# A new written order, column halves and earlier weight loads in the first block of a fused attention, FFN and MoE kernel

## The chip, the cores and the metric

One core of one Trainium2 chip runs the whole program. The metric is device time in microseconds (us) of one execution, as a median of several runs. Engines: PE is TensorE, DVE is VectorE, ACT is ScalarE, POOL is GpSimd; SP only issues DMAs. Each engine works through its own queue of instructions strictly in order, and semaphores tie the queues together.

## What is computed

Sliding-window attention with a few global keys (2 batches, 8 heads, 768 tokens, head size 64), then an FFN with the gate h * tanh(softplus(h)), then four experts, weighted by probabilities. All inputs are float32, except the FFN's weights, which come as float64.

```python
scores = scale * np.matmul(q, k.transpose(0, 1, 3, 2))
keep = is_global | is_local          # 8 global keys, 96 local ones
scores = np.where(keep, scores + bias, -1e9)
a = np.exp(scores - np.max(scores, axis=-1, keepdims=True))
a = a / (np.sum(a, axis=-1, keepdims=True) + 1e-09)
x = np.matmul(a, v)                  # -> 1536 x 512
h = x @ w_in                         # 512 -> 2048
y = (h * np.tanh(np.log1p(np.exp(h)))) @ w_out
for e in range(4):                   # experts, 512 -> 1024 -> 512
    out += p[:, e:e + 1] * (np.maximum(y @ w1[e], 0.0) @ w2[e])
```

## The kernel before

The 1536 tokens are worked on in three blocks of 512. In blocks 1 and 2 attention is spread over the FFN and expert steps of the block before, and every matmul of the FFN and the experts is done in three products of split operands. The first block is different, and it is where the change lies: attention has nothing to hide behind there, and the block runs in plain float32 products (each matmul instruction shows as two records). Its attention is cut into 16 pairs of heads (`FirstPair`, four pairs for each 128 tokens; the first four look at 128 keys, the others at 256), and its FFN into 16 steps of 128 hidden units.

`first_block` (line 786 on) issues all this from a string, `PLAN`, one letter for each operation, taken from left to right. So the string is the order of every engine's queue. The letters, with the engine and the line in the profile:

- of a pair: S scores (PE, L355), X bias and row minimum (DVE, L264, two instructions), E exponential with row sum (ACT, L275, two), D reciprocals for two pairs (DVE, L366 and L367), N scaling by the reciprocal (POOL, L372, two), T transposes (PE, L192), C copy of the transposed tile out of PSUM by ACT (L382), Z the same by DVE (not used before), A values (PE, L391), and for each four pairs F or G, the copy of the result into `x0` by ACT or DVE (L396; G alone is used before)
- of the conversion of one FFN weight tile from float64 bits to float32: a (ACT, L584), then three t (DVE, L587, L589, L591; the last one also sends the tile to a DRAM copy, `wfirst`, through SP, L593)
- of an FFN step: H hidden product (PE, L750, 8 records), e, c, n, l, u, m, v, g the gate (e: ACT, L643; c and n: DVE, L650 and L657; l: ACT, L662 and L663; u, m, v, g: DVE, L667, L672, L678, L682), P projection (PE, L762, 8 records)
- w: a third of the splitting of an expert tile (ACT L609 for the first third, DVE L612 for the two others), Y: matmuls that keep PE busy, i: the loads for the next block's attention, j and 1 to 6: its first round.

H needs all 16 pairs copied into `x0` and the converted tile; P needs the gate's g. A FFN weight tile is loaded (1 MB) into one of four buffers, so the load of tile k is issued on SP when tile k-4 has been converted (`ahead`, L802, calls `fetch`, L557); the tiles 12 to 15 use only two of the buffers. SP's queue is in order too: a load stands behind the DRAM copies and loads that were put there before it. The first two tiles are loaded at the start, between the tiles of keys and queries (L131 to L137). The three expert tiles that the block needs at its end are loaded by the first w (L856).

The values lie in `vz` as 192 columns for each pair and 128 keys: 64 of the one head, 64 of zeros, 64 of the other. Each matmul of A takes 128 of them (L391), so both heads' products go to all 128 output rows and the zeros keep them apart. Scores, by contrast, use the array in two halves of 64 rows, one for each head.

The flag that chooses between the narrow and the general program is worked out from two integers, loaded by two DMAs, one on SP and one on ACT (L68, L69).

Of the kernel before, what the change touches and what calls it, by code (L numbers as in the profile page):

```python
# [41 lines left out]
PLAN = (  # L42
    "SSYXXESYSEXSEDXNXESNTDCTXSENANCTXESACTDEAXNSCNETXACTDEGANCSNaAXatTTtCSCAEXtAESDGNSXNTXEStTCDSEXNACNX"
    "EAtaTDTtNCSCANXEtAEtTTCGCADatNAaNtTtCTACtaAtGtHattteHacntlteHuamcvgnPetlctauHtmvngtlPteaucmHtvngtlPt"
    "eaucmHtvgntlPteaucmtHvngtlPteaucmtHvgntltPeucmtvHngtltPeucmtvHngtltaPeucmvngHtltautiPemcvgnPtltutHmw"
    "vwgwePwcnwlwHumvgePcnlHuwmwvwgeHcnlPuemcvngHlumvPegcnlPumvgj1P23456"
)
# [12 lines left out]
@with_exitstack  # L60
def fused_attention_ffn_moe(ctx: ExitStack, tc: tile.TileContext, qkv, qk, vz, q_t, k_t, v_n, nloc, nglob, wff, wts, probs, out):
    nc = tc.nc
# [4 lines left out]
    nw = const.tile([P, 2], I64, tag="nw", name="nw")  # L67
    nc.sync.dma_start(nw[:, 0:1], nloc.unsqueeze(0).broadcast_to([P, 1]))  # L68
    nc.scalar.dma_start(nw[:, 1:2], nglob.unsqueeze(0).broadcast_to([P, 1]))  # L69

# [61 lines left out]
    for n, raw in enumerate(raws):  # L132
        at = slice(P if n < 2 else 0, 3 * P)
        nc.sync.dma_start(raw[:, 0:6 * P].rearrange("p (n c) -> p n c", n=2)[:, :, at],
                          qk[2 * n:2 * n + 2, :, at].rearrange("n p c -> p n c"))
        if wff.dtype == I64 and n % 2:
            nc.sync.dma_start(big[n // 2].bitcast(I64), wff[n // 2])  # L137

# [183 lines left out]
class FirstPair(NarrowPair):  # L322
# [6 lines left out]
    def load(self):  # L329


        nc, body, n = self.nc, self.body, self.n // 2
        if self.n % 2 == 0:
            v = body.ring.tile([P, 1024], F32, tag="wl" if n % 2 else "wh", name=f"vz{n}")[:, 0:768]
            v = body.values = v.rearrange("p (n c d) -> p n c d", n=2, c=2)
            c = slice(2 - self.nk, 2)
            nc.sync.dma_start(v[:, :, c, :], body.vz[n][:, :, c, :])
            if n < len(body.raws):
                qk = body.raws[n]
            else:  # L340
                qk = body.wpool.tile([P, 1024], F32, tag="w", name=f"qk{n}")
            body.keys = qk[:, 0:6 * P].rearrange("p (n c) -> p n c", n=2)
            if n >= len(body.raws):
                nc.sync.dma_start(body.keys, body.qk[2 * n:2 * n + 2].rearrange("n p c -> p n c"))
        self.v = body.values[:, self.n % 2]
        self.k, self.q = body.keys[:, self.n % 2, 0:2 * P], body.keys[:, self.n % 2, 2 * P:3 * P]
# [21 lines left out]

    def scale(self):
        for j in range(2):  # L370
            p = self.p[:, j, 0:self.nk * P]
            self.nc.gpsimd.tensor_scalar(p, p, self.sum[:, j:j + 1], 0.0, ALU.mult, ALU.add)  # L372

# [10 lines left out]
    def av(self):  # L384

        body = self.body
        if self.pr == 0:
            body.o = body.bank(f"o{self.u}", 1)
        mms = [(c, j) for c in range(self.nk) for j in range(2)]
        for c, j in mms:  # L390
            self.nc.tensor.matmul(body.o[:, self.pr * P:(self.pr + 1) * P], self.v[:, 2 - self.nk + c, j * 64:j * 64 + P],  # L391
                                  self.pt[:, c * 256 + j * P:c * 256 + (j + 1) * P], start=(c, j) == mms[0], stop=(c, j) == mms[-1])

# [129 lines left out]
class Body:  # L523
# [33 lines left out]
    def fetch(self, s):  # L557

        kind, t, n = self.steps[s]
        if kind == "ffn" and self.wide and t == 0:  # L560
            self.w64[s] = (self.big + self.twice)[TURN[n]].bitcast(I64)
            if n > 1 or not self.loaded:
                self.nc.sync.dma_start(self.w64[s], self.wff[n])
            return
        if kind == "ffn" and self.wide and t > self.first:
            return
        self.w32[s] = self.wpool.tile([P, 1024], F32, tag="w", name=f"w{s}")
        self.nc.sync.dma_start(self.w32[s], (self.wts if kind == "moe" else self.wfirst if self.wide else self.wff)[n])
# [219 lines left out]
    def first_block(self, ready, now):  # L788
# [10 lines left out]
        for pair in pairs:  # L799
            pair.load()  # L800

        def ahead():  # L802
# [18 lines left out]

        def scale(k):
            assert n["D"] > k // 2
            pairs[k].scale()

# [6 lines left out]

        def hidden(s):
            assert n["F"] == 4 and n["t"] >= 3 * s + 3
            self.accumulating = True
            self.hidden_first(s)
            ahead()
# [14 lines left out]
        def part(k):  # L852
            c, third = divmod(k, 3)
            assert ready["fetch"] >= NF1 and n["S"] == len(pairs) and n["P"] >= 8 + 2 * c
            if third == 0:
                now("fetch", NF1 + 3)  # L856
                next(parts[c])
# [5 lines left out]
        def begin_next(k):  # L863
# [4 lines left out]
        ops = {  # L868
            "S": scores, "X": pair("biased"), "E": pair("exps"), "D": inverse, "N": scale, "T": pair("trans"),
            "C": pair("copy", nc.scalar.copy), "Z": pair("copy", nc.vector.tensor_copy), "A": pair("av"),  # L870
# [6 lines left out]
        }  # L877
        same = dict(Z="C", G="F")
        for token in PLAN:
# [170 lines left out]
```

## Time and profile before

| | us |
|---|---|
| median of 3 runs | 945.83 (945.04 to 948.88) |
| profiled execution, time | 944.16 |
| its span, first to last instruction | 942.3 |
| first H of the block starts | 49.23 |
| last P of the block ends | 167.7 |

The profiled execution has 1.86 us outside its span and lies 1.67 us under the median. PE is busy for 97% of the span. The rows further down show the first 167.7 us stage by stage; behind them the program runs for 774.6 us that the change does not touch.

### The profile page before, as it was taken

To read this page: it belongs to the slowest core of one execution; us is meant where nothing else is said; L and a number is where in the kernel's file an instruction comes from. 1 tells how busy PE (TensorE), PEld (TensorE's weight loads), DVE (VectorE), ACT (ScalarE), POOL (GpSimd) and SP (SyncE) were. 2 spreads that over 40 slices of the span, in tenths; PEclk is the share of its full clock that TensorE was granted. 3 is DMA by queue.
4 is the path that set the end of the run, shared out by engine and by line. 5 is a ranking of instruction groups with operands and counts; after the bars stand their busy time and mean duration, and the time that the engine had idled before them with its cause. 6 is when DMAs were issued, how large, how long until landed. Compare 5 with 4: busy or idle time off the path is not lost.

```text
span 942.3 us, 11540 instructions
## 1 busy us (share of the span) xinstructions
PE 910.1 (97%) x3962; PEld 697.8 (74%) x3962; DVE 527.8 (56%) x1041; ACT 440.5 (47%) x860; POOL 379.6 (40%) x391
## 2 busy tenths in 40 slices
PE   8899979999899999999999999999999999999997
PEld 4744434787678888877777888888888888888886
DVE  4889957777673178888777621228886121112122
ACT  4844324776663256556776642323445332432330
POOL 3500000577575444437666754400004454454450
PEclk7999999999999999999999999999999999999999
DMA  8876450543312478863435223044562342323301
GB/s 308 296 284 224 160 196 1 201 157 134 112 68 90 156 263 298 296 261 134 143 126 201 69 90 106 29 178 179 195 252 94 107 134 99 103 90 97 105 23 49
DMA packets 40517, 143.88 MB, mean 153 GB/s; under 512 B 4736, under 2 KB 7552, under 8 KB 38400
## 3 DMA queue, kind: packets, MB, share of 16 engines
q1 hardware_dynamic: 40160, 143.02, 42.6%
q8 instruction: 33, 0.54, 0.2%
q14 instruction: 36, 0.29, 0.1%
q10 hardware_dynamic: 288, 0.03, 0.0%
HBM read 114.71 MB, written 28.31 MB: 152 GB/s over the span
## 4 chain that ended last, share of the span: by engine, by line
PE 71%; DVE 15%; ACT 8%; issue 2%; DMA 2%; POOL 0%; SPq 0%; ACTq 0%; DVEq 0%
PE h L627 29%; PE acc L733 28%; PE acc L762 5%; PE h L750 4%; DVE kl L231 2%; ACT p L275 1%; DVE nr L672 1%; PE o L297 1%; ACT wh L609 1%; DVE e L667 1%; PE pt L192 1%; DVE nr L678 1%; DVE n L655 1%; DVE e L682 1%; DVE n L648 1%
## 5 line engine op out<-in xcount | busy, mean ns | idle before, releaser
L612 POOL TENSOR_TENSOR wl<-w,wh 128x512 fp32r<-128x512 f32 x218 | 290.2, 1352 | 324.2 <-ACT wh L609 314.6
L708 DVE SCALAR_TENSOR_TENSOR gl<-h,gh 128x512 fp32r<-128x512 f32 x96 | 66.2, 689 | 267.3 <-ACT gh L703 267.3
L609 ACT CAST wh<-w 128x1024 fp32r<-128x1024 f32 x112 | 117.7, 1050 | 121.8 <-PE acc L733 106.2
L733 PE MATMUL acc<-wh,gh 128*128 128x512 f32 (+1 forms) x384 | 151.4, 394 | 0.0
L733 PE MATMUL acc<-wh,gl 128*128 128x512 f32 (+1 forms) x384 | 148.9, 388 | 0.0
L733 PE MATMUL acc<-wl,gh 128*128 128x512 f32 (+1 forms) x384 | 148.7, 387 | 0.0
L703 ACT ACTIVATE gh<-h 128x512 fp32r<-128x512 f32 x96 | 57.3, 597 | 114.4 <-PE h L627 114.4
L733 PEld LDWEIGHTS acc<-wh,gl 128*128 128x128 f32 x384 | 72.1, 188 | 15.1
L733 PEld LDWEIGHTS acc<-wl,gh 128*128 128x128 f32 x384 | 72.2, 188 | 14.1
L733 PEld LDWEIGHTS acc<-wh,gh 128*128 128x128 f32 x384 | 72.2, 188 | 14.0
L240 POOL TENSOR_TENSOR v<-raw,v 128x256 fp32r<-128x256 f32 x32 | 26.9, 841 | 116.6 <-ACT v L239 116.6
L750 PE MATMUL h<-x,w 128*128 128x512 f32 x128 | 57.2, 593 | 0.8 <-DVE x L396 0.8
L187 POOL TENSOR_SCALAR p<-p,st 128x256 f32<-128x256 f32 (+1 forms) x64 | 29.9, 479 | 66.5 <-DVE st L185 65.6
L627 PE MATMUL h<-y0h,wh 128*128 128x512 f32 x128 | 52.6, 411 | 2.5 <-DVE st L264 1.5
L275 ACT ACTIVATE p<-t,st 128x256 f32<-128x256 f32 (+1 forms) x96 | 46.4, 486 | 17.5 <-DVE st L264 16.5
L627 PE MATMUL h<-y1h,wh 128*128 128x512 f32 x128 | 50.7, 396 | 0.1
L627 PE MATMUL h<-y0h,wl 128*128 128x512 f32 x128 | 50.5, 395 | 0.0
L627 PE MATMUL h<-y0l,wh 128*128 128x512 f32 x128 | 50.4, 394 | 0.0
L627 PE MATMUL h<-y1l,wh 128*128 128x512 f32 x128 | 49.9, 390 | 0.0
L733 PE MATMUL acc<-gh,wh 128*128 128x512 f32 x128 | 49.9, 390 | 0.0
L627 PE MATMUL h<-y1h,wl 128*128 128x512 f32 x128 | 49.9, 390 | 0.0
L627 PE MATMUL h<-y2h,wh 128*128 128x512 f32 x128 | 49.9, 390 | 0.0
(152 smaller groups left out, 1821.3 us busy)
## 6 DMA issues: line engine op xcount, KB each, us to landing
w<-in_wts SPq DMA_DIRECT2D x96, 512.0 KB, 3.5
raw<-in_qkv SPq DMA_DIRECT2D x32, 512.0 KB, 3.9
big<-in_wff SPq DMA_DIRECT2D x10, 1024.0 KB, 5.9
wfirst<-w SPq DMA_DIRECT2D x16, 512.0 KB, 3.0
w<-wfirst SPq DMA_DIRECT2D x16, 512.0 KB, 4.2
wkeep<-wh SPq DMA_DIRECT2D x16, 512.0 KB, 3.1
wkeep<-wl SPq DMA_DIRECT2D x16, 512.0 KB, 2.9
wh<-wkeep SPq DMA_DIRECT2D x16, 512.0 KB, 3.2
```

The lines of the kernel that those rows point to most:

```text
L187: nc.gpsimd.tensor_scalar(self.p[:, j, 0:self.nk * P], self.p[:, j, 0:self.nk * P], st[:, 2 + j:3 + j], 0.0, ALU.mult, ALU.add)
L231: nc.vector.tensor_tensor(self.kl, self.k, self.kh.bitcast(F32), ALU.subtract)
L240: nc.gpsimd.tensor_tensor(vv[:, :, 1:3, :], v, vv.bitcast(F32)[:, :, 0:4:3, :], ALU.subtract)
L275: nc.scalar.activation(p[:, j, 0:n], t[:, j, 0:n], AF.Exp, bias=self.least[:, j:j + 1], scale=-1.0, accum_out=self.sum[:, j:j + 1])
L609: (nc.vector.tensor_copy if copy == "vector" else nc.scalar.copy)(hi, w)
L612: getattr(nc, engine or "gpsimd").tensor_tensor(lo[:, c], w[:, c], hi.bitcast(F32)[:, c], ALU.subtract)
L627: nc.tensor.matmul(ps, a[:, c], r[:, kc, :], start=m == 0, stop=m == 3 * KC - 1)
L703: self.nc.scalar.activation(gh, self.h[s], AF.Relu)
L708: nc.vector.scalar_tensor_tensor(gl, h, 0.0, gh.bitcast(F32), ALU.max, ALU.subtract)
L733: nc.tensor.matmul(acc[:, h], a, r, start=f == 0 and m == 0, stop=f == per - 1 and m == 2)
L750: self.nc.tensor.matmul(ps, self.w32[s][:, kc * P:(kc + 1) * P], self.x0[:, kc, :], start=kc == 0, stop=kc == KC - 1)
L762: self.nc.tensor.matmul(acc, w[:, 512 + d * P:512 + (d + 1) * P], g, start=s == 0, stop=s == NF1 - 1)
```

## The change

`PLAN` is a new order of the same operations, with five changes of engine or kind: 8 of the 16 copies of transposed tiles go from ACT to DVE (Z for C), 6 of the 16 scalings from POOL to DVE (V for N), the 4 copies into `x0` from DVE to ACT (F for G). Before the first H stood 14 t and 6 a; now 4 t and 4 a stand there, the rest after it. The pieces w stand later. The three expert tiles are loaded at the fifth H instead of the first w. Of the two FFN tiles of the start the first is loaded after all four tiles of keys and queries, the second after the loads of the tenth pair. `vz` loses its zeros, and each A takes 64 columns and writes 64 output rows. The two integers come in one DMA.

```diff
 PLAN = (
-    "SSYXXESYSEXSEDXNXESNTDCTXSENANCTXESACTDEAXNSCNETXACTDEGANCSNaAXatTTtCSCAEXtAESDGNSXNTXEStTCDSEXNACNX"
-    "EAtaTDTtNCSCANXEtAEtTTCGCADatNAaNtTtCTACtaAtGtHattteHacntlteHuamcvgnPetlctauHtmvngtlPteaucmHtvngtlPt"
-    "eaucmHtvgntlPteaucmtHvngtlPteaucmtHvgntltPeucmtvHngtltPeucmtvHngtltaPeucmvngHtltautiPemcvgnPtltutHmw"
-    "vwgwePwcnwlwHumvgePcnlHuwmwvwgeHcnlPuemcvngHlumvPegcnlPumvgj1P23456"
+    "SSYXXESYSEXSEDXNXESNTDCTXSENAZNEXATTSCZEDAXANSFSNEXTTDCNEZAXANTETSCZaADXNAtSFNTEXSCTXEAZSEDAVSVaXTTX"
+    "CSEZAEADVVFTXTCEZAAaDVVTtTCaAZtAFtHtttteHcatntlHteaumcvnegacPtltumtHvngtlPteuamvcHgntltaPeucmtvgHntl"
+    "tauPetmvgcPntltauHtmvgtePcnatltHutmteHvcagntltPeumavgHcntltuPetmcvnHgtlutPmevgcntlPumvgHtttePtcnlHau"
+    "mtvtaHgetictnPetlcutHmwvgnwlPweuwcmvgHnwlwuwmPevcgnwlwPumvgj1P23456"
 )
...
-    nc.sync.dma_start(nw[:, 0:1], nloc.unsqueeze(0).broadcast_to([P, 1]))
-    nc.scalar.dma_start(nw[:, 1:2], nglob.unsqueeze(0).broadcast_to([P, 1]))
+    nc.sync.dma_start(nw, nums.unsqueeze(0).broadcast_to([P, 2]))
...
-        if wff.dtype == I64 and n % 2:
-            nc.sync.dma_start(big[n // 2].bitcast(I64), wff[n // 2])
+    if wff.dtype == I64:
+        nc.sync.dma_start(big[0].bitcast(I64), wff[0])
...
-            v = body.ring.tile([P, 1024], F32, tag="wl" if n % 2 else "wh", name=f"vz{n}")[:, 0:768]
+            v = body.ring.tile([P, 1024], F32, tag="wl" if n % 2 else "wh", name=f"vz{n}")[:, 0:512]
...
-    def scale(self):
+    def scale(self, engine):
         for j in range(2):
             p = self.p[:, j, 0:self.nk * P]
-            self.nc.gpsimd.tensor_scalar(p, p, self.sum[:, j:j + 1], 0.0, ALU.mult, ALU.add)
+            engine.tensor_scalar(p, p, self.sum[:, j:j + 1], 0.0, ALU.mult, ALU.add)
...
-        mms = [(c, j) for c in range(self.nk) for j in range(2)]
-        for c, j in mms:
-            self.nc.tensor.matmul(body.o[:, self.pr * P:(self.pr + 1) * P], self.v[:, 2 - self.nk + c, j * 64:j * 64 + P],
-                                  self.pt[:, c * 256 + j * P:c * 256 + (j + 1) * P], start=(c, j) == mms[0], stop=(c, j) == mms[-1])
+        for c in range(self.nk):
+            for j in range(2):
+                r = slice(j * 64, (j + 1) * 64)
+                self.nc.tensor.matmul(body.o[r, self.pr * P:(self.pr + 1) * P], self.v[:, 2 - self.nk + c, r],
+                                      self.pt[:, c * 256 + j * P:c * 256 + (j + 1) * P], start=c == 0, stop=c == self.nk - 1)
...
         if kind == "ffn" and self.wide and t == 0:
             self.w64[s] = (self.big + self.twice)[TURN[n]].bitcast(I64)
-            if n > 1 or not self.loaded:
+            if n > 0 or not self.loaded:
                 self.nc.sync.dma_start(self.w64[s], self.wff[n])
...
         for pair in pairs:
             pair.load()
+            if pair.n == 9:
+                now("fetch", 2)
...
         def hidden(s):
+            if s == 4:
+                for c in range(NF1, NF1 + 3):
+                    self.fetch(c)
...
             if third == 0:
-                now("fetch", NF1 + 3)
+                ready["fetch"] = NF1 + 3
                 next(parts[c])
```

## Rows read from the trace of the kernel before

**Rows 1.** Windows, by stages: length, then busy us (instructions), granted clock, DMA

```profile
core 0: us, PE busy (x) PEld busy (x) DVE busy (x) ACT busy (x) POOL busy (x), PEclk, DMA share, GB/s
8.81:18.41 9.60, 9.60 (x33) 4.80 (x33) 5.62 (x33) 5.08 (x21) 3.27 (x8) 0.50 1.03 385
18.41:49.23 30.82, 27.46 (x206) 21.83 (x205) 24.82 (x70) 25.69 (x71) 16.20 (x27) 1.00 0.87 318
49.23:61.20 11.97, 10.57 (x25) 4.51 (x25) 10.05 (x14) 4.91 (x7) 0.00 (x0) 1.00 0.93 326
61.20:123.09 61.89, 61.89 (x145) 27.36 (x146) 60.61 (x85) 26.02 (x37) 0.00 (x0) 1.00 0.58 207
123.09:136.64 13.55, 8.60 (x18) 3.59 (x16) 7.57 (x13) 3.73 (x5) 0.00 (x0) 0.87 0.52 207
136.64:167.70 31.06, 31.06 (x75) 13.84 (x74) 20.33 (x34) 12.06 (x21) 0.73 (x1) 1.00 0.07 23
167.70:942.30 774.60, 756.38 (x3465) 620.18 (x3463) 396.14 (x783) 361.72 (x701) 357.78 (x345) 1.00 0.40 140
```

**Rows 2.** Timeline of PE: start, length, what; in brackets the idle time before

```profile
49.23 10.57 PE L750 MATMUL h<-x,w 128*128 128x512 f32 x24 [0.79 <-DVE x L396]
61.20 3.67 PE L762 MATMUL acc<-gh,w 128*128 128x512 f32 x8 [1.40 <-DVE gh L682]
...
131.63 5.17 PE L762 MATMUL acc<-gh,w 128*128 128x512 f32 x8 [4.95 <-DVE gh L682]
...
164.10 3.60 PE L762 MATMUL acc<-gl,w 128*128 128x512 f32 x8
```

**Rows 3.** Timeline of all engines around the idle time at 126.7 us

```profile
123.70 1.73 SPq L568 DMA_DIRECT2D w<-in_wts  x3
129.21 1.04 ACT L609 CAST wh<-w 128x1024 fp32r<-128x1024 f32 x1 [8.23 <-DMA w<-in_wts]
...
130.90 0.68 DVE L682 TENSOR_TENSOR gh<-r,h 128x512 f32<-128x512 f32 x1
```

**Rows 4.** Tile nw: time from issue to landing of its two loads

```profile
DMA to landing us min/median/max: 4.8/5.1/5.5
```

**Rows 5.** Groups by form, 8.8 to 49.3 us: busy us, mean ns, idle before

```profile
L372 POOL TENSOR_SCALAR p<-p,st 128x256 f32<-128x256 f32 x24 | 15.5, 662 | 11.3 <-DVE st L367 5.0 <-PE pt L192 4.2 <-PE o L391 2.2
L391 PE MATMUL o<-pt,vz 128*128 128x128 f32 x112 | 15.2, 283 | 0.0
...
L382 ACT COPY pt<-pt 128x512 f32<-128x512 f32 x12 | 6.7, 580 | 3.2 <-PE pt L192 3.1
...
L584 ACT ACTIVATE w<-big 128x1024 f32<-128x1024 f32 x4 | 4.5, 1161 | 0.0
...
L396 DVE COPY x<-o 128x512 f32<-128x512 f32 x4 | 2.7, 672 | 0.9 <-PE o L391 0.9
```

**Rows 6.** Groups by form, 49.23 to 167.7 us, the conversion on DVE

```profile
L591 DVE SCALAR_TENSOR_TENSOR w<-big,w 128x1024 int32<-128x1024 int32 x8 | 9.8, 1223 | 0.2
L589 DVE SCALAR_TENSOR_TENSOR w<-big,w 128x1024 int32<-128x1024 int32 x8 | 9.8, 1222 | 0.1
...
L587 DVE TENSOR_SCALAR w<-w 128x1024 int32<-128x1024 int32 x11 | 7.6, 687 | 0.0
```

**Rows 7.** Timeline of DVE at the start, a scaling of 256 columns

```profile
7.87 0.33 DVE L115 TENSOR_SCALAR dist<-rel,nlg 128x256 f32<-128x256 f32 x1
```

**Rows 8.** Timeline of PE, window of 30 ns at 25.00 us

```profile
25.01 0.49 PE L355 MATMUL s<-qk 64*128 64x256 f32 x2
```

**Rows 9.** Timeline of PE from 24.9 us: scores, then values, then transposes

```profile
25.01 0.70 PE L355 MATMUL s<-qk 64*128 64x256 f32 x4
25.64 1.16 PE L391 MATMUL o<-pt,vz 128*128 128x128 f32 x8
26.64 1.04 PE L192 MATMUL pt<-ident,p 128*128 128x128 f32 x8
```

**Rows 10.** DMA issues, 47 to 57 us: loads of FFN tiles, median us to landing

```profile
big<-in_wff SPq DMA_DIRECT2D x2, 1024.0 KB, 8.6
```

**Rows 11.** The same, 64 to 90 us

```profile
big<-in_wff SPq DMA_DIRECT2D x2, 1024.0 KB, 5.7
```

More of the change, by code (lines that the diff above doesn't have):

```diff
@@ L60, in fused_attention_ffn_moe @@
 @with_exitstack
-def fused_attention_ffn_moe(ctx: ExitStack, tc: tile.TileContext, qkv, qk, vz, q_t, k_t, v_n, nloc, nglob, wff, wts, probs, out):
+def fused_attention_ffn_moe(ctx: ExitStack, tc: tile.TileContext, qkv, qk, vz, q_t, k_t, v_n, nums, wff, wts, probs, out):
     nc = tc.nc
@@ L820, in inverse, with scale, run @@
             pairs[2 * k].inverse()
-        def scale(k):
-            assert n["D"] > k // 2
-            pairs[k].scale()
+        def scale(engine):
+            def run(k):
+                assert n["D"] > k // 2
+                pairs[k].scale(engine)
+            return run
         def take(engine):
@@ L868, in first_block @@
         ops = {
-            "S": scores, "X": pair("biased"), "E": pair("exps"), "D": inverse, "N": scale, "T": pair("trans"),
+            "S": scores, "X": pair("biased"), "E": pair("exps"), "D": inverse, "N": scale(nc.gpsimd), "V": scale(nc.vector), "T": pair("trans"),
             "C": pair("copy", nc.scalar.copy), "Z": pair("copy", nc.vector.tensor_copy), "A": pair("av"),
@@ L877, in first_block @@
         }
-        same = dict(Z="C", G="F")
+        same = dict(Z="C", G="F", V="N")
         for token in PLAN:
@@ L1017 @@
                          for j in range(2)], axis=1)
-    vz = np.zeros((n0 // 2, P, 2, 2, 192), q.dtype)
-    v0 = qkv[0, 0:TB // P].reshape(n0 // 2, 2, P, 1024)[:, :, :, 768:1024].reshape(n0 // 2, 2, P, 2, 2, 64)
-    vz[..., 0:64] = v0[..., 0, :].transpose(0, 2, 1, 3, 4)
-    vz[..., 128:192] = v0[..., 1, :].transpose(0, 2, 1, 3, 4)
+    vz = first[:, :, :, 768:1024].reshape(n0 // 2, 2, P, 2, P).transpose(0, 2, 1, 3, 4)
     w_in, w_out = np.asarray(inputs["moe_w_in"]), np.asarray(inputs["moe_w_out"])
@@ L1038 @@
         "qkv": qkv.reshape(B * NT * NP, P, 1024), "qk": qk, "vz": vz, "q_t": q_t, "k_t": k_t, "v_n": v_n,
-        "nloc": np.asarray(inputs["n_local"], np.int64).reshape(1), "nglob": np.asarray(inputs["n_global"], np.int64).reshape(1),
+        "nums": np.concatenate([np.asarray(inputs[n], np.int64).reshape(1) for n in ("n_local", "n_global")]),
         "wff": wff, "wts": wts, "probs": probs,
```

## The prediction

> **What bounds the kernel now.** I read the windows by stages first, because the share of 97% for PE is a mean over a stretch that the change does not touch (774.6 us from 167.70 on) and one of 167.7 us that it does [rows 1]. In the first the same instructions follow in the same order, so I give it no change. In the second the reader is to see four stages with four limits. From 8.81 to 18.41 PE works at the lower of its two clocks (0.50) and the other engines wait for it. From 18.41 to 49.23, the attention, no engine is full: PE 27.46, ACT 25.69 and DVE 24.82 of 30.82 us. From 49.23, where the first H starts, to 123.09 DVE is the fullest (10.05 of 11.97, 60.61 of 61.89), and PE is fed just in time; it then stands still once and has DVE far ahead of it to the end (20.33 of 31.06). So DVE is short of time before 123 us and idle after it: that imbalance is what an order can use.
>
> Then the timeline of PE, for the places where it stood still [rows 2]: 1.40 us before the first P, where the first gate is a chain without cover, and 4.95 us before the P at 131.63, which then ran at 5.17 instead of 3.60 us because the clock fell in the pause (0.87 in that stage [rows 1]). The timeline of all engines shows why: the expert tiles were issued only at 123.70, the ACT copy of the first one waited 8.23 us for its landing, and behind it in ACT's queue stood the exponential that the gate needs [rows 3]. PE's own work is 32 groups of H and P; 145 records of 8 to a group fill 61.89 us from 61.20 to 123.09, that is 18 groups of 3.44 us [rows 1], together 110.1 us. The block takes 118.5 us from the first H to the end.
>
> **The start.** Two loads of the integers become one on SP. The two took 4.8 and 5.5 us [rows 4], and the flag, the biases and all that follows hang on it. With the shorter time all starts 0.7 us earlier; the bounds are 0 (the one load takes the longer time) and 0.7. I take 0.7.
>
> **Up to the first H.** DVE is costed first, since it is what the new order loads. Eleven of the fourteen t go behind the first H (t3 is issued before it but holds nothing up): four of 0.687 and seven of 1.223 us, 11.3 us [rows 6]. The four copies into x0 go to ACT: 4 x 0.672 = 2.7 us [rows 5]. Eight copies of transposed tiles come to DVE; no row has this copy on DVE, and the nearest is the copy into x0, also 512 columns out of PSUM: 6 x 0.672 and two of half the size, 4.7 us. Six scalings come, two instructions each; the nearest row is a scaling of 256 columns from the start, 0.33 us [rows 7], so 12 x 0.33 = 4.0 us (below that 0.25 is possible, above it 0.66, what POOL takes for one [rows 5]: 3 to 8 us). Net 14.0 - 8.7 = 5.3 us less. DVE was idle for 4.0 + 6.0 us from 8.81 to 49.23 [rows 1]. If that idle time stays, H starts at 49.2 - 0.7 - 5.3 = 43.2.
>
> PE: the values took 112 records at 0.125 us (eight from 25.64 to 26.64 [rows 9]), 14.0 us. The halved form has no row; the nearest is the scores, where each head uses half the array's rows, and there two records of 0.48 us begin within 30 ns of each other [rows 8], so the two heads run side by side. If the halves of columns do the same, 7.0 us go; if they do not, nothing goes. I take 7.0, and then PE's 27.46 us become 20.5. The Trainium skill speaks against a part of that: "TensorEngine Tiling (Array Packing)", Tiling Modes, says that a change of the tiling mode drains the engine, and the new order has about nine changes between transposes or H and the halved values that were none before. By the trace such a change costs little: eight values right behind the scores last 0.88 us from first to last start, against 7 x 0.111 without a change, so 0.1 us, and nine of them 1 us; by a full drain of a matmul's length, 0.28, it would be 2.5 us. Either leaves PE ahead of DVE here.
>
> ACT loses eight copies (6 x 0.58 and two smaller, 4.2 us) and two a of 1.16, and gets four copies of 0.58; 25.69 becomes 21.5 [rows 1, 5]. POOL loses six of its scalings, which on average took 0.66 us [rows 5]. So PE and ACT would be done by about 39, and DVE stays last. With both lighter, a little of DVE's idle time should go; I put **the first H at 43.0**, 6.2 us earlier.
>
> The loads: `vz` is a third smaller, and the first FFN tile no longer stands ahead of keys 2 and 3. The second FFN tile now stands ahead of the last three pairs of `vz` and keys, 1 MB at 385 GB/s [rows 1], 2.7 us; before, it stood ahead of all of them, so nothing gets later. Cost nothing; if it did hold up the eleventh pair, at most 2.7 us.
>
> **After the first H.** What left DVE before it comes back here, under PE's long products. DVE has 45 t, 96 gate instructions and 6 w; the 85 instructions of the same mix from 61.20 to 123.09 took 60.61 us, 0.713 each [rows 1], so 147 x 0.713 = 104.8 us. That is close to PE's 110.1, of which the last P (3.44) needs the last gate. So DVE is what sets the end, as far as it waits. From 49.23 to 123.09 it was idle for 3.2 of 73.9 us [rows 1], at that rate 4.9 over 112 us. To that come the loads of the FFN tiles: tile k is now asked for when tile k-4 is done, at most five or six t before its a. A lone load lands in 5.7 us [rows 11], one in a burst in 8.6 [rows 10]; just after the first H four conversions follow each other closely, and there I expect one such burst, 2.9 us, a part of it under the first gate's wait. I take 7 us of idle time in all (bounds 4 and 14). The expert tiles, 1.5 MB, stand in SP's queue behind the fifth copy to DRAM; they put the next FFN tile back by 1.5 MB at 326 GB/s [rows 1], 4.6 us once, about two thirds of a step, which the tiles in hand cover; without that cover it would be up to 3 us. The pause of 4.95 us and the 1.57 us of low clock behind it go, and DVE's 6.0 us of idle time in that stage with them [rows 1, 2]; next late is the gate, not a load. The first gate stays a bare chain, so 1.4 us before the first P stay.
>
> End of the block: 43.0 + 104.8 + 7.0 + 3.4 = 158.2, against 167.7: **9.5 us earlier**. By PE alone it would be 43.0 + 110.1 + 1.4 = 154.5, which is the floor of this reckoning.
>
> **The sum.** 944.16 - 9.5 = 934.7 for an execution like the profiled one; it lies 1.67 under the median of the runs, so 936.3, rounded to 936.
>
> **Rivals.**
> The halves of columns do not run side by side. For: no row shows them, and there may be drains. Against: the halves of rows do [rows 8]. PE would keep 27.46 us of work from 17.7 on, and with 1.5 us of waits H would start at 46.6, 3.6 us later than forecast: 940.
>
> The gain is given back: DVE waits after the first H for more than I think, 14 to 20 us instead of 7 (it was 19.9 from 49.23 to 167.70, nearly all of it after 123 [rows 1]). For: DVE has 6.0 us more work than before (8.7 - 2.7), and now no slack at the end. Against: its idle time had one named cause, the late expert load, and the slack of the end. 943 to 947, within 0.5% of before.
>
> Slower: **the four-buffer ring sets the pace after the first H**. Twelve loads (tiles 4 to 15) are asked for only after a conversion, and each a stands in ACT's queue ahead of the l that DVE's gate waits for. If every load lands like those in a burst, 8.6 instead of 5.7 us, with a cover of about 7, each costs DVE 1.5 us, 18 in all beside the 4.9: 22.9 instead of 7, the block ends at 174.1 and the time is 952. The turning point is 0.8 us for each load: 7 us of idle time may grow by the 9.5 us of the gain, over twelve loads. For: the bursts in the trace. Against: 1.5 MB for a step of 6.9 us is 218 GB/s, far under the 326 of the burst, so the queue should not stay full.
>
> **How the numbers follow.** Forecast 0.61 (its own range 931.5 to 939.5), the halves not side by side 0.17, given back 0.14, slower 0.08. The range of 931.5 to 944.0 takes in the forecast down to near the PE floor (930.8 + 1.7), the 940, the dear scalings (+4) and the half of the third case. Of the measurement I say only that 0.5%, 4.7 us, is about what it can tell. Faster by more than that (under 941.1): the forecast and nearly all of the second case, 0.77; within it 0.15; slower 0.08.
>
> **What would show it.** In the profile after: the first H at about 43, with the records of the two heads' values starting in pairs; if they start 0.11 us apart, the second rival holds its ground. No wait of ACT for `in_wts` near 125 us and no fall of the clock there. DVE busy for nearly all of the stage after the first H up to the last P, with about 7 us of idle time; waits of ACT for `in_wff` well over 1 us each, again and again, would be the ring. The last P should end near 158, and the 774.6 us behind it should be as they were; if they are not, the forecast is wrong in what it leaves out.

## The result and the profile after

The changed kernel takes 933.06 us (median of 4, 932.88 to 934.25); the kernel before, run beside it, 947.3 (median of 4). The ratio is 0.9859 (95%: 0.9833 to 0.9886). In the later runs the kernel before had medians of 944.8 to 945.3, so the gain is 12 to 14 us. From one profiled execution to the other it is 9.9 us: 944.16 before, 934.25 after, span 932.4. The forecast was 934.7 for such an execution and 936 for the median. The other 2 to 4 us of the medians' gain lie in how far a profiled execution is from its median, and no row shows them: before it lay under the median, after it is the slowest of the four.

The windows by stages of the kernel after show where that lies (length, busy us and instructions of each engine, granted clock, DMA); they answer to [rows 1]:

```profile
core 0: us, PE busy (x) PEld busy (x) DVE busy (x) ACT busy (x) POOL busy (x), PEclk, DMA share, GB/s
6.37:39.32 32.95, 27.72 (x236) 17.61 (x236) 25.82 (x109) 26.89 (x83) 10.05 (x22) 1.00 0.65 240
39.32:153.40 114.08, 109.33 (x249) 47.33 (x249) 104.27 (x148) 46.83 (x68) 0.73 (x1) 0.99 0.59 217
153.40:157.00 3.60, 3.60 (x9) 1.69 (x10) 3.51 (x7) 1.76 (x3) 0.00 (x0) 1.00 0.40 126
157.00:932.40 775.40, 757.53 (x3465) 621.24 (x3463) 396.55 (x783) 361.83 (x701) 357.90 (x345) 0.99 0.40 140
```

The first block now ends at 157.0 instead of 167.7. Behind it next to nothing happened: 775.4 against 774.6 us. Inside the block the gain is almost all ahead of the first H, which starts 9.9 us earlier (39.32 against 49.23); from there to the end of the last P it takes 117.7 us, against 118.5.

The timeline of PE in the kernel after, beside [rows 2]:

```profile
6.37 0.71 PE L353 MATMUL s<-raw 64*128 64x128 f32 x8 [0.60 <-DVE dist L115]
...
26.43 0.66 PE L391 MATMUL o<-pt,vz 128*64 128x128 f32 x8
27.02 0.70 PE L353 MATMUL s<-qk 64*128 64x256 f32 x4
27.65 0.33 PE L391 MATMUL o<-pt,vz 128*64 128x128 f32 x2
...
39.32 10.57 PE L750 MATMUL h<-x,w 128*128 128x512 f32 x24 [0.69 <-ACT x L396]
52.43 5.26 PE L762 MATMUL acc<-gh,w 128*128 128x512 f32 x8 [2.54 <-DVE gh L682]
57.52 3.60 PE L750 MATMUL h<-x,w 128*128 128x512 f32 x8
...
153.40 3.70 PE L762 MATMUL acc<-gl,w 128*128 128x512 f32 x8 [0.65 <-DVE gl L682]
```

The first scores start at 6.37 instead of 8.81. The pause of 4.95 us that stood before the P at 131.63 has no successor there; the largest left behind the first H is 2.54 us before the first P, where the clock fell (the P takes 5.26 us instead of 3.60):

```profile
52.00:53.00 1.00, 0.57 (x1) 0.50 (x2) 0.75 (x3) 0.49 (x2) 0.00 (x0) 0.61 0.24 98
53.00:54.00 1.00, 1.00 (x2) 0.33 (x1) 1.00 (x1) 0.00 (x0) 0.00 (x0) 0.50 0.14 57
```

(Windows of 1 us, same columns; the granted clock, third from the end, goes to 0.50.)

Three of the prices that had no row, in the groups by form of the kernel after, 6.3 to 39.3 us (busy us, mean ns, idle before): the halved values, the copy of transposed tiles on DVE (Z), the scaling on DVE (V).

```profile
L391 PE MATMUL o<-pt,vz 128*64 128x128 f32 x112 | 8.6, 285 | 1.0 <-ACT pt L380 0.7 <-DVE pt L380 0.3
...
L380 DVE COPY pt<-pt 128x512 f32<-128x512 f32 x6 | 4.1, 690 | 1.3 <-PE pt L191 1.3
...
L370 DVE TENSOR_SCALAR p<-p,st 128x256 f32<-128x256 f32 x12 | 3.4, 350 | 0.2
```

And the landing of the one load of the integers, from the view of that tile, beside the 4.8 and 5.5 us of [rows 4]:

```profile
DMA to landing us min/median/max: 3.1/3.1/3.1
```

### The profile page after: what moved, and what is told of

Read it like the earlier page. It is cut to its first block, busy times and chain, and to the rows that moved or that the text cites. A ratio compares the mean times of both kernels' runs of the same rounds, so it can differ in the third digit from the quotient of the medians.

```text
span 932.4 us, 11519 instructions
## 1 busy us (share of the span) xinstructions
PE 902.5 (97%) x3962; PEld 689.6 (74%) x3962; DVE 532.8 (57%) x1057; ACT 438.6 (47%) x856; POOL 370.3 (40%) x379
## 4 chain that ended last, share of the span: by engine, by line
PE 64%; DVE 19%; ACT 8%; DMA 4%; issue 3%; SPq 0%; POOL 0%; ACTq 0%; DVEq 0%; POOLq 0%
PE h L627 30%; PE acc L733 29%; DMA raw<-in_wff 2%; DVE kl L230 2%; DVE nr L672 2%; DVE e L667 2%; PE o L296 1%; DMA big<-in_wff 1%; ACT p L274 1%; PE pt L191 1%; DVE nr L678 1%; DVE w L589 1%; DVE n L655 1%; DVE e L682 1%; ACT wh L609 1%
## 5 line engine op out<-in xcount | busy, mean ns | idle before, releaser
L703 ACT ACTIVATE gh<-h 128x512 fp32r<-128x512 f32 x96 | 57.3, 597 | 115.7 <-PE h L627 115.7
L274 ACT ACTIVATE p<-t,st 128x256 f32<-128x256 f32 (+1 forms) x96 | 46.3, 484 | 13.7 <-DVE st L263 13.3
```

What stands on the lines that cost most here:

```text
L274: nc.scalar.activation(p[:, j, 0:n], t[:, j, 0:n], AF.Exp, bias=self.least[:, j:j + 1], scale=-1.0, accum_out=self.sum[:, j:j + 1])
L703: self.nc.scalar.activation(gh, self.h[s], AF.Relu)
```

## The experiments

Two questions were open: which part brings the gain, and whether the written order, on which the forecast rested most, brings any. Four kernels add one part to the kernel before or exchange the order in the kernel after; three undo one part in the kernel after; five test causes that came up on the way. All numbers stand here together; "first S" (the first scores), "first H" and "H to end" (from the first H to the end of the block's last P) are from the one profiled execution of each kernel, the ratio is that of the times to the kernel before, run beside it.

| kernel | median us | ratio (95%) | first S | first H | H to end |
|---|---|---|---|---|---|
| before | 944.8 to 947.3 | 1 | 8.81 | 49.23 | 118.5 |
| after | 933.06 | 0.9859 (0.9833 to 0.9886) | 6.37 | 39.32 | 117.7 |
| e1_one_load | 946.27 | 1.0008 (0.9991 to 1.0025) | 6.53 | 49.76 | 123.4 |
| h1_load_order | 942.47 | 0.9980 (0.9966 to 0.9994) | 6.83 | 45.66 | 120.1 |
| e2_halves | 944.3 | 0.999 (0.997 to 1.001) | 8.95 | 47.42 | 121.4 |
| e3_early_experts | 938.56 | 0.9924 (0.9901 to 0.9947) | 8.90 | 48.27 | 114.6 |
| e4_old_order | 934.08 | 0.9887 (0.9862 to 0.9913) | 6.47 | 44.02 | 113.2 |
| f1_two_loads | 936.83 | 0.9907 (0.9884 to 0.9931) | 9.34 | 42.98 | 116.5 |
| f2_full_columns | 935.94 | 0.9904 (0.9879 to 0.9929) | 6.49 | 42.86 | 115.3 |
| f3_late_experts | 939.11 | 0.9940 (0.9921 to 0.9959) | 6.40 | 37.80 | 122.9 |
| k1_old_engines | 937.60 | 0.9923 (0.9906 to 0.9940) | 6.61 | 44.17 | 116.9 |
| f4_load_first | 932.66 | 0.9860 (0.9834 to 0.9887) | 6.88 | 39.09 | 117.1 |
| g1_gate_first | 932.77 | 0.9874 (0.9857 to 0.9890) | 6.44 | 38.76 | 115.7 |
| g2_old_order_dve | 935.79 | 0.9906 (0.9892 to 0.9921) | 6.53 | 44.12 | 113.1 |

Two things limit how finely this table can be read. f3_late_experts differs from the kernel after only behind the first H, and still its first H comes 1.5 us sooner: places of two executions can differ by that much without a cause in the kernel. And only the ratios were taken against runs made beside each kernel; the kernel after has four runs of its own, beside which the kernel before had 947.3. Differences to the kernel after are therefore given by medians and by ratios where the two part.

### One load of the integers

In the kernel before:

```diff
-    nc.sync.dma_start(nw[:, 0:1], nloc.unsqueeze(0).broadcast_to([P, 1]))
-    nc.scalar.dma_start(nw[:, 1:2], nglob.unsqueeze(0).broadcast_to([P, 1]))
+    nc.sync.dma_start(nw, nums.unsqueeze(0).broadcast_to([P, 2]))
```

> The kernel before, with the two integers in one load and nothing else changed. Theory A (the load's landing sets the start): the changed kernel's load landed after 3.14 us, where the two of before took 4.77 and 5.50, and its first score came 2.4 us earlier; if the joining does that, the first score here starts near 6.4 instead of 8.8, PE's clock does not fall in the pause before it, and the time is 2.4 to 4 us less. Theory B (the landing differs from execution to execution by chance): the two kernels' times agree within 1 us.

The scores start 2.3 us earlier, but the time does not move. Its profiled execution was the slowest of its twelve (951.05), so only places are read from it, and its 123.4 us from the first H to the end carry that. The timeline of PE:

```profile
6.53 0.71 PE L354 MATMUL s<-raw 64*128 64x128 f32 x8 [0.61 <-DVE dist L115]
...
20.93 0.70 PE L354 MATMUL s<-qk 64*128 64x256 f32 x4 [2.68 <-DMA qk<-in_qk]
...
49.76 10.57 PE L749 MATMUL h<-x,w 128*128 128x512 f32 x24 [0.78 <-DVE x L395]
```

PE gets ahead and then waits 2.68 us for a tile of keys. The windows up to that wait and behind it point to the cause: up to it the DMA queue is full, at the same rate as in the first row of [rows 1]. Behind it the granted clock is 0.94 in the mean, so PE lost some of its speed too.

```profile
6.53:20.90 14.37, 9.14 (x56) 5.59 (x57) 7.61 (x43) 9.98 (x39) 5.85 (x14) 1.00 1.03 388
20.90:49.76 28.86, 25.48 (x180) 20.93 (x180) 23.07 (x60) 20.75 (x50) 13.62 (x20) 0.94 0.77 283
```

### The order of the first loads

To the kernel before, the one load and the change's order of loads:

```diff
-        if wff.dtype == I64 and n % 2:
-            nc.sync.dma_start(big[n // 2].bitcast(I64), wff[n // 2])
+    if wff.dtype == I64:
+        nc.sync.dma_start(big[0].bitcast(I64), wff[0])
...
-            if n > 1 or not self.loaded:
+            if n > 0 or not self.loaded:
...
+            if pair.n == 9:
+                now("fetch", 2)
```

> The kernel before, with one load of the integers and the changed kernel's order of loads (the first FFN tile behind all four tiles of keys and queries, the second behind the loads of the tenth pair); old string, padded values. One load alone brought the first score 2.3 us earlier and nothing in time. Theory A (the queue of loads, full from 6 to 32 us, sets the attention's pace, and an earlier start only waits for keys): with the FFN tiles out of the way the early keys land 2 to 3 us sooner, the scores wait less than 1 us in all for in_qk, the first H starts 1.5 to 3 us earlier than in the kernel with one load alone and the time is 1.5 to 3 us under it. Theory B (DVE and PE set the pace): the first H stays at 49 to 50 and the time at that of before.

Against e1_one_load the time falls by 3.8 us by the medians and 2.6 by the ratios, whose intervals just touch, and the first H comes 4.1 us earlier. The third and fourth tile of keys no longer stand behind the first FFN tile of 1 MB, and the keys of the ninth and tenth pair not behind the second. The timeline of PE still shows a wait for keys, of 2.02 us where under 1 was expected, but 2.6 us earlier:

```profile
18.32 0.70 PE L354 MATMUL s<-qk 64*128 64x256 f32 x4 [2.02 <-DMA qk<-in_qk]
...
45.66 10.57 PE L749 MATMUL h<-x,w 128*128 128x512 f32 x24 [0.78 <-DVE x L395]
```

The other 1.5 us come behind that wait, and the window from there to the first H shows a difference beside the loads: the clock stays at 1.00, where it was 0.94 in e1_one_load.

```profile
18.32:45.66 27.34, 23.97 (x181) 19.29 (x181) 22.98 (x60) 20.65 (x50) 13.65 (x20) 1.00 0.94 363
```

### The same start, undone in the kernel after

```diff
-    nc.sync.dma_start(nw, nums.unsqueeze(0).broadcast_to([P, 2]))
+    nc.sync.dma_start(nw[:, 0:1], nums[0:1].unsqueeze(0).broadcast_to([P, 1]))
+    nc.scalar.dma_start(nw[:, 1:2], nums[1:2].unsqueeze(0).broadcast_to([P, 1]))
```

> The changed kernel with the two integers in two loads again. Theory A (the joining sets the start): first score 2 to 2.5 us later than in the changed kernel, time 2.4 to 4 us more than its 933.1 us. Theory B (the landing of 3.14 us has another cause: the other loads of the start, or chance): within 1 us of 933.1.

The two loads land after 5.1 and 6.0 us (view of the tile), the scores start at 9.34, and the first H at 42.98, 3.7 us later than in the kernel after; the median is 3.8 us above it (4.5 by the ratios).

```profile
DMA to landing us min/median/max: 5.1/5.6/6.0
```

The clock may be part of that: in the window from the first scores on, PE runs at 0.50.

```profile
9.34:14.60 5.26, 5.26 (x16) 2.43 (x16) 3.38 (x19) 3.83 (x15) 1.37 (x3) 0.50 0.53 188
```

In all kernels with one load it landed in 3.0 to 3.4 us, in all with two they took 4.7 to 6.0. All four kernels with two loads have such a stretch at 0.50 between 8 and 19 us; no kernel with one load has one there. So the joining gave no gain that can be told under the old order of loads, and under the new one it is worth the 3.0 us of the earlier first scores and some more; how much of that is the start and how much the clock was not separated.

### Halves of columns

In the kernel before, the change's values and its `vz` without zeros:

```diff
-            v = body.ring.tile([P, 1024], F32, tag="wl" if n % 2 else "wh", name=f"vz{n}")[:, 0:768]
+            v = body.ring.tile([P, 1024], F32, tag="wl" if n % 2 else "wh", name=f"vz{n}")[:, 0:512]
...
-        mms = [(c, j) for c in range(self.nk) for j in range(2)]
-        for c, j in mms:
-            self.nc.tensor.matmul(body.o[:, self.pr * P:(self.pr + 1) * P], self.v[:, 2 - self.nk + c, j * 64:j * 64 + P],
-                                  self.pt[:, c * 256 + j * P:c * 256 + (j + 1) * P], start=(c, j) == mms[0], stop=(c, j) == mms[-1])
+        for c in range(self.nk):
+            for j in range(2):
+                r = slice(j * 64, (j + 1) * 64)
+                self.nc.tensor.matmul(body.o[r, self.pr * P:(self.pr + 1) * P], self.v[:, 2 - self.nk + c, r],
+                                      self.pt[:, c * 256 + j * P:c * 256 + (j + 1) * P], start=c == 0, stop=c == self.nk - 1)
```

> The kernel before, with the values in halves of columns, without zeros, old order. Theory A (the forecast: DVE is last before the first H, PE has room): the values' records start in pairs, PE's work before the first H falls by about 6.5 us, but the first H comes at most 1 us earlier; time 0 to 1 us less. Theory B (PE bounds the attention also in the old order): the first H comes 4 to 6 us earlier and the time is 4 to 6 us less.

The values cost PE less, but the time does not move by what can be told (0.997 to 1.001). The first H comes 1.8 us earlier, where at most 1 was expected, and this is lost again behind it: the clock fell (first H 12.23 instead of 10.57 us), and the pause for the expert tiles is 5.84 instead of 4.95 us. Ahead of it PE waits 3.4 us for POOL (2.4 in the kernel before) and 1.4 for keys (none there). The timeline of PE:

```profile
47.42 12.23 PE L751 MATMUL h<-x,w 128*128 128x512 f32 x24 [0.80 <-DVE x L397]
...
132.25 5.62 PE L763 MATMUL acc<-gh,w 128*128 128x512 f32 x8 [5.84 <-DVE gh L683]
```

The reverse edit in the kernel after:

> The changed kernel with the values in full columns over zeros, and so with the larger vz. Theory A (in the new order the halves make room on PE): PE's work before the first H grows by about 6.5 us and the first H comes 2 to 4 us later, as the second rival of the prediction has it; time 935 to 937. Theory B (PE has room either way): within 1 us of 933.1.

Here it is worth 2.9 us (4.3 by the ratios), and the first H comes 3.5 us later. The groups of this kernel, against 8.6 us of the kernel after:

```profile
L390 PE MATMUL o<-pt,vz 128*128 128x128 f32 x112 | 14.9, 283 | 0.8 <-ACT pt L380 0.8
```

So PE's work in the attention is on the path in the new kernel; in the old one, waits for POOL and for keys and a lower clock took its place.

### Early expert tiles

In the kernel before:

```diff
         def hidden(s):
+            if s == 4:
+                for c in range(NF1, NF1 + 3):
+                    self.fetch(c)
...
-                now("fetch", NF1 + 3)
+                ready["fetch"] = NF1 + 3
```

> The kernel before, with the three expert tiles loaded at the fifth H. Theory A (the pause of 4.95 us and the 1.57 us of low clock behind it hang on that load alone): the pause is gone, 6 to 6.5 us less. Theory B (the order puts other waits there, or the 1.5 MB push the loads of FFN tiles back): a pause of 2 us or more stays near 127 us, at most 3 us less.

This part alone brings 0.76% (7.2 us). In the timeline of PE the first P's wait is the only one left after the first H:

```profile
48.27 10.57 PE L750 MATMUL h<-x,w 128*128 128x512 f32 x24 [0.78 <-DVE x L396]
61.34 5.37 PE L762 MATMUL acc<-gh,w 128*128 128x512 f32 x8 [2.50 <-DVE gh L682]
```

The reverse edit in the kernel after:

> The changed kernel with the expert tiles loaded at the first w. In the new order the first w comes after the last conversion, so the load has less DVE work before it than in the old one. Theory A (the load is the pause): ACT waits 5 us or more for in_wts behind the first w, PE stands still for 3 us or more, and the time is 4 to 7 us more than 933.1. Theory B (the new order has enough work between the load and its use): within 1 us.

It costs 6.0 us (7.7 by the ratios). The old pause comes back under the new order, first on ACT, then on PE (timelines of the two):

```profile
141.95 1.04 ACT L609 CAST wh<-w 128x1024 fp32r<-128x1024 f32 x1 [10.32 <-DMA w<-in_wts]
```

```profile
147.36 5.40 PE L762 MATMUL acc<-gl,w 128*128 128x512 f32 x8 [4.54 <-DVE gl L682]
```

### The written order

The kernel after with the four lines of the old `PLAN`, so with the old order and the old engines, and with all else new.

> The changed kernel with the old string of letters: everything but the order and its changes of engine. Theory A (the parts add up): one load, halves and early experts together give 7 to 10 of the about 13 us, and the order the rest, 3 to 6 us. Theory B (only the new order turns the parts into time): at most 4 us less than before.

It takes 934.08 us, 1.0 more than the kernel after (2.6 by the ratios), and the intervals of the ratios overlap. Neither expectation held: the parts bring 10.7 us, and the order with its engines adds less than the 3 to 6 of the first theory. The windows up to the first H and from there to the end of the block (columns as in the table of windows above), first of this kernel:

```profile
6.47:44.02 37.55, 31.50 (x238) 19.07 (x237) 30.48 (x103) 30.21 (x89) 19.49 (x34) 0.90 0.94 344
44.02:157.20 113.18, 113.18 (x258) 50.01 (x259) 98.47 (x144) 47.16 (x69) 0.73 (x1) 0.97 0.48 180
```

then of the kernel after, whose window up to the first H stands above:

```profile
39.32:157.00 117.68, 112.93 (x257) 49.02 (x258) 107.78 (x154) 48.58 (x71) 0.73 (x1) 0.99 0.59 214
```

The new order has the first H 4.7 us earlier and takes 4.5 us longer behind it; the blocks end at 157.2 and 157.0. In the old order PE never pauses after the first H: its work is the bound there, and DVE is idle for 14.7 of 113.18 us. In the new order DVE has 9.3 us more to do there, of which 4.8 go into its idle time (9.9 left), and PE pauses for 4.75 us, nearly all of it before a P that waits for a gate of DVE's. Two groups of PE's timeline in this kernel show what the old order still loses: a wait for POOL ahead of the first H, and a first H group of 13.64 instead of 10.57 us at a lower clock.

```profile
35.58 0.55 PE L191 MATMUL pt<-ident,p 128*128 128x128 f32 x3 [1.09 <-POOL p L370]
...
44.02 13.64 PE L750 MATMUL h<-x,w 128*128 128x512 f32 x24 [0.79 <-DVE x L396]
```

### The engines

The kernel after with its new string, but V written as N, Z as C, F as G:

```diff
-    "SSYXXESYSEXSEDXNXESNTDCTXSENAZNEXATTSCZEDAXANSFSNEXTTDCNEZAXANTETSCZaADXNAtSFNTEXSCTXEAZSEDAVSVaXTTX"
-    "CSEZAEADVVFTXTCEZAAaDVVTtTCaAZtAFtHtttteHcatntlHteaumcvnegacPtltumtHvngtlPteuamvcHgntltaPeucmtvgHntl"
+    "SSYXXESYSEXSEDXNXESNTDCTXSENACNEXATTSCCEDAXANSGSNEXTTDCNECAXANTETSCCaADXNAtSGNTEXSCTXEACSEDANSNaXTTX"
+    "CSECAEADNNGTXTCECAAaDNNTtTCaACtAGtHtttteHcatntlHteaumcvnegacPtltumtHvngtlPteuamvcHgntltaPeucmtvgHntl"
```

> The changed kernel with its new string, but each letter on its old engine: all scalings on POOL, all copies of transposed tiles on ACT, the copies into x0 on DVE. DVE has about 6 us less work before the first H, ACT and POOL more. Theory A (the moves free the attention of POOL, which the conversions on DVE block, and of ACT's queue): the first H starts 2 to 4 us later than in the changed kernel (39.3), and the time is 2 to 4 us over its 933.1. Theory B (DVE is what sets the end of the block, and the moves only load it): the time is 1 to 4 us under 933.1. If the moves only shift work about: within 1 us.

937.6 us: the changes of engine (three kinds of letter, not five) are worth 4.5 us by the medians, and the new string without them is 3.5 us slower than the old one, with intervals that overlap a little. Which of the three moves brings how much was not tried. The timeline of POOL shows the price of a scaling beside DVE's conversions (L589 and L591 run on DVE from 36.12 to 38.73): four take 3.60 us there, 1.85 elsewhere.

```profile
32.58 1.86 POOL L370 TENSOR_SCALAR p<-p,st 128x256 f32<-128x256 f32 x4 [2.27 <-ACT pt L380]
36.40 3.60 POOL L370 TENSOR_SCALAR p<-p,st 128x256 f32<-128x256 f32 x4 [1.96 <-ACT pt L380]
```

PE then waits for them and works at a lower clock up to the first H (timeline of PE):

```profile
39.13 1.81 PE L191 MATMUL pt<-ident,p 128*128 128x128 f32 x7 [1.09 <-POOL p L370]
...
44.17 12.82 PE L750 MATMUL h<-x,w 128*128 128x512 f32 x24 [0.80 <-DVE x L396]
```

The Trainium skill, "SBUF — State Buffer" (two separate sides), says that GpSimd and VectorE share a pair of ports, that a VectorE operation with two SBUF inputs may take it, and that the other engine then stands still. The rows agree: both conversions read two tiles, and the scalings beside them took twice their time.

If only those last scalings were the trouble of the old order, moving the last four of them to DVE there should have cured it (with the edit of f4_load_first, below, in the same kernel):

```diff
-    "EAtaTDTtNCSCANXEtAEtTTCGCADatNAaNtTtCTACtaAtGtHattteHacntlteHuamcvgnPetlctauHtmvngtlPteaucmHtvngtlPt"
+    "EAtaTDTtVCSCAVXEtAEtTTCGCADatVAaVtTtCTACtaAtGtHattteHacntlteHuamcvgnPetlctauHtmvngtlPteaucmHtvngtlPt"
```

> The changed kernel with the old string, the last four scalings on DVE instead of POOL, and the load of each FFN tile ahead of the DRAM copy. In the old string under the other parts PE had no pause after the first H, but 3.4 us of pauses for POOL scalings before it and a stretch of low clock from 36.6 to 50.3. Theory A (POOL, blocked by the conversions on DVE, makes the pauses and they the low clock): both go, the first H starts near 42, the block ends near 153, and the time is 929 to 931, under the new order's. Theory B (what DVE takes over costs as much): 933 to 935.

It did not. The first H stays at 44.12, and the wait now names DVE (timeline of PE): where many conversions stand among the last pairs, the scalings are late on either engine. That this is the conversions' doing is my reading of the order and was not tried.

```profile
39.11 1.55 PE L191 MATMUL pt<-ident,p 128*128 128x128 f32 x8 [1.77 <-DVE p L370]
44.12 13.54 PE L748 MATMUL h<-x,w 128*128 128x512 f32 x24 [1.56 <-DVE x L396]
```

### The ring of FFN tiles

In the kernel after, ACT waits 17.9 us in all for FFN tiles up to 157 us (9.1 in the kernel before). The view of its waits shows them by buffer (us, count, longest), the timeline of ACT the longest:

```profile
ACT w L584 <- DMA big<-in_wff: 13.9, 8, 2.8
...
ACT w L584 <- DMA raw<-in_wff: 4.0, 3, 2.1
```

```profile
46.46 1.18 ACT L584 ACTIVATE w<-big 128x1024 f32<-128x1024 f32 x1 [2.80 <-DMA big<-in_wff]
```

Here the next FFN load is put ahead of the DRAM copy in SP's queue:

```diff
-        if self.first:
-            nc.sync.dma_start(self.wfirst[s], m)
...
-        def ahead():
+        def ahead(extra=0):
...
-                if n["S"] < FREE.get(TURN[c], 0) or any(n["t"] < 3 * m + 3 for m in before):
+                if n["S"] < FREE.get(TURN[c], 0) or any(n["t"] + extra < 3 * m + 3 for m in before):
...
-            ahead()
+            ahead(1)
+            if k % 3 == 2:
+                nc.sync.dma_start(self.wfirst[c], self.w32[c])
```

> The changed kernel, with the load of the next FFN tile put in SP's queue ahead of the DRAM copy of the tile just converted, instead of behind it. Theory A (after the first H the four-buffer ring costs time: ACT waited 17.9 us in all for in_wff, and the gate stands behind it): each load lands about 1.4 us sooner, the pause before the first P falls under 2 us, DVE's idle time after the first H falls by 3 to 5 us, and the time is 1 to 3 us less than 933.1. Theory B (DVE and PE are full anyway, the waits of ACT cost nothing): within 0.5 us of 933.1.

By the view of the DMA issues the loads into `big` just after the first H (39 to 62 us) land after 5.8 us, in the kernel after after 7.5, and PE's wait before the first P falls to 1.58 us; the clock holds. First f4_load_first, then the kernel after:

```profile
big<-in_wff SPq DMA_DIRECT2D x3, 1024.0 KB, 5.8
```

```profile
big<-in_wff SPq DMA_DIRECT2D x2, 1024.0 KB, 7.5
```

The time does not change (932.66 against 933.06), and DVE's idle time behind the first H falls only from 9.9 to 9.3 us, where 3 to 5 less were expected. In g1_gate_first the first gate also comes ahead of a conversion. The string from the first H to the third:

```diff
-HcatntlHteaumcvnegacPtltumtH
+HctntlaHteumcvnegcaPtlatumtH
```

> The changed kernel with the load of each FFN tile ahead of the DRAM copy, and in the string the first three a behind the first two l (ctntla, umcvnegca, latumt), so that ACT does not wait for a tile while a gate waits for ACT. Theory A (after the first H the waits of ACT for in_wff hold up the gates): the first P starts about 1.3 us after the third H ends instead of 2.5, the clock stays up, PE's pauses after the first H fall from 4.7 to about 2.5 us, and the time is 2 to 4 us under 933.1. Theory B (DVE's sum sets the end): the early P come sooner, later ones later, and the time is within 1 us of 932.7, that of the load put first alone.

The profiled block ends 2.5 us sooner than after's, but it is the fastest of four executions and after's is the slowest of four; the median, 932.77, cannot be told from the kernel after. So no cost of these waits for loads can be told (0.3 to 0.4 us by the medians, in intervals some 3 to 5 us wide), and no version here clearly beats the changed kernel. The timeline of PE in g1_gate_first:

```profile
50.91 3.67 PE L760 MATMUL acc<-gh,w 128*128 128x512 f32 x8 [1.58 <-DVE gh L680]
...
111.26 3.70 PE L760 MATMUL acc<-gl,w 128*128 128x512 f32 x8 [1.07 <-DVE gl L680]
```

### Where the gain comes from

In the old order, by the ratios to the kernel before at 945 us: expert tiles 7.2 us, one load with its load order 1.9, halves 0.9 (an interval that takes in 1). Together 10.0; e4_old_order, which has these parts and neither the new order nor its engines, gained 10.7. What the new order with its engines adds is 1.0 us by the medians and 2.6 by the ratios, within overlapping intervals. In the new order, undoing one part costs by the medians 3.8 (one load, with the load order left new), 2.9 (halves) and 6.0 (expert tiles), 12.7 together, about the whole gain; by the ratios 4.5, 4.3 and 7.7, 16.4 together, more than the 13.3 of the whole, so the parts cannot simply be added. The start and the halves are worth more there. My reading is that the new order makes the attention a stage that can use them; it gives most of its earlier first H back behind it.

## Why the prediction was right, and where its steps were not

The number held in part by luck, because two steps missed in opposite directions: the first H came 3.7 us earlier than forecast, and the rest of the block took 2.5 us longer. Block's end: forecast 158.2, measured 157.0. The median was 3 us under the forecast of 936, mostly because the 1.67 us by which the profiled execution had lain under the median were added again; this time it lay 1.2 above. (The floor of the range is 944.16 - 13.2 = 931.0, not 930.8; nothing hangs on it.)

**The start** was the step with the worst bound: 0.7 us, with 0 and 0.7 as ends, measured 2.44. I took the shorter of the two old loads as the price of the one load. But neither old load was alone; the single one takes 3.1 us, 1.7 less than the shorter. PE then keeps its clock, too: the stretch at 0.50 that opened [rows 1] is gone. Why one load lands so much sooner than either of two was not tried.

**The attention.** The terms of DVE's sum were right: V 0.350 (0.33 forecast), Z 0.690 (0.672); DVE's busy time from the first scores to the first H went from 30.44 to 25.82 us, 4.6 less (5.3 forecast). What failed was "if that idle time stays": it fell from 9.98 to 7.13 us. The first H was at 39.32 instead of 43.0: 1.7 us of the difference come from the start, the other 2 from here.

**The loads "cost nothing".** That step failed. The DMA share of 1.03 at 385 GB/s stood in the first row of [rows 1], and I read that row for its clock alone. In the kernel before PE never waited for keys; as soon as it started earlier it did, for 2.68 us (e1_one_load). The order of loads is worth 2.6 to 3.8 us there (h1_load_order against e1_one_load), and without it no gain from the earlier start can be told.

**Halves.** Right: two heads' records start within 30 ns, and PE's values fell from 15.2 to 8.6 us, 6.6 of the 7.0. The change of mode is nearly as cheap as I took it: between the start of the eight values at 26.43 and the scores at 27.02 lie 0.59 us, against 4 x 0.111 for four pairs, so 0.15 for a change and some 1.3 us for nine. A drain of a matmul's length, 0.28, as I had worked out from the rule of the Trainium skill ("TensorEngine Tiling (Array Packing)", Tiling Modes), does not show. The rival's price for the opposite case was also right: 3.6 us forecast, 3.5 measured in f2_full_columns.

**After the first H** the sum was 104.8 busy + 7.0 idle + 3.4 for the last P = 115.2. Measured: 104.27 + 9.81 + 3.60 = 117.7. So the busy time was right within 0.5 us, and the idle time was inside its bounds of 4 and 14 but 2.8 over. The groups of DVE in the kernel after, 39.3 to 157 us, put 6.4 us of it on ACT's part of the gate, and only 0.8 on a converted tile that was late. Late loads could still stand behind ACT's part, but with the loads sooner it stays at 6.7 us (f4_load_first), so they explain little of it.

```profile
L667 DVE SCALAR_TENSOR_TENSOR e<-n,r 128x512 f32<-128x512 f32 x16 | 11.0, 689 | 6.4 <-ACT r L663 6.4
...
L587 DVE TENSOR_SCALAR w<-w 128x1024 int32<-128x1024 int32 x15 | 10.3, 688 | 0.8 <-ACT w L584 0.8
```

The 1.4 us before the first P became 2.54, and the clock fell in it; I had taken this pause as fixed. In ACT's queue ahead of it stands a conversion that waits 2.80 us for its load; with the loads sooner (f4_load_first) the pause is 1.58 us.

**The imbalance that an order can use** was the idea of the forecast, and it brought little. By the forecast's own terms, 0.7 us for the start and 6.5 for the expert tiles, 2.3 of its 9.5 us were left for the order with its engines and the halves together; the order with its engines measured 1.0 by the medians, 2.6 by the ratios (e4_old_order). DVE was indeed idle after 123 us, for 16.7 us [rows 1], and only 5.7 of them hung on the late expert tiles (groups of DVE in the kernel before, 49.23 to 167.7 us):

```profile
L612 DVE TENSOR_TENSOR wl<-w,wh 128x512 fp32r<-128x512 f32 x6 | 4.0, 686 | 5.7 <-ACT wh L609 5.7
```

With them early the idle time is still there, 14.7 us from the first H on, but PE is full (113.18 of 113.18 us) and sets the end. By the trace ten more t run there in the new order. About half of their time finds room in that idle time; the rest makes gates late, for which PE then waits: 4.7 us gained ahead of the first H, 4.5 paid behind it.

**Expert tiles.** Right: 6.5 us were forecast for the pause and the low clock behind it; 7.2 measured by adding the part (e3_early_experts), 6.0 by undoing it (f3_late_experts).

**Rivals.** Halves one after the other, and the gain given back (DVE idle 14 to 20 us), did not happen. The ring did what it was feared for only on ACT: eleven waits of 1.6 us in the mean, 17.9 together. That was the sign named for the ring, and it was no good sign, for by f4_load_first and g1_gate_first no time can be told to hang on it.

## What to carry to other kernels

Read the DMA share of a stage before costing anything in it: where it stands at 1, an earlier start may only meet the loads sooner, as here, until their order is changed. Undo each part of a joint change as well as adding it alone; here the halves could not be told from nothing in the old order and were worth 2.9 us in the new. Before moving work into an engine's idle time, look at the engine that is full beside it: here PE set the end, and half of what was moved came back as pauses of PE.

## What was not expected of the hardware

- One load of both integers to 128 partitions lands after 3.1 us, two loads of one integer each, on two queues, after 4.7 to 6.0; the first tile of keys then lands at 4.7 instead of 7.3 us.
- The granted clock fell from 1.00 to 0.50 (2.4 and 1.2 GHz) during a pause of PE of 2.54 us (at 52.2 in the kernel after) and did not in one of 1.58 us at the same place (f4_load_first, g1_gate_first). In e4_old_order and k1_old_engines it fell in the attention, where no single pause of PE near it was over 1.1 us, and stayed at 0.50 for 13.7 and 10.2 us.
